# A fused attention and two-layer feed-forward kernel: the second layer's input weights kept as two words, its output weights split on VectorE

## The chip, the cores and the metric

The program runs on one core of one Trainium2 chip. The metric is the device time of one execution in microseconds (us); lower is better. The engines are TensorE (PE, with PEld for its weight loads), VectorE (DVE), ScalarE (ACT), GpSimd (POOL) and SyncE (SP), which issues almost all DMAs from one in-order queue.

## The reference, cut to what matters

```python
def _attn_ref(q, k, v, tau):                      # 4 x 8 heads, 576 rows of 64
    scores = scale * np.matmul(q, k.transpose(0, 1, 3, 2))
    scores = np.where(scores >= np.max(scores, -1, keepdims=True) - tau, scores, -1e9)
    ... softmax ...
    return np.matmul(attn, v)

def _moe_ref(x, w_in, w_out, g_ln):               # 2304 tokens, 512 -> 1024 -> 512
    h = x @ w_in
    solu = h * softmax(h)
    ln = (solu - mean) / sqrt(var + 1e-6) * g_ln
    return ln @ w_out

def _moe2_ref(x, w_in, w_out):                    # 2304 tokens, 512 -> 2048 -> 512
    h = x @ w_in
    g = h * np.tanh(log1p(exp(h)))
    return g @ w_out
```

The output is `_moe2_ref(_moe_ref(_attn_ref(...)))`. The change lies in the weights of `_moe2_ref`, called W2_in and W2_out here.

## The kernel before

**Precision.** A float32 product is made of three products of a shorter matmul type: every operand is split into a high word (a rounding copy, made by ScalarE) and a low word (operand minus high word), and high by high, low by high and high by low are summed.

**The second feed-forward layer** multiplies 2 by 2 blocks with seven products instead of eight (Strassen's scheme in Winograd's form). So each group of 256 columns of W2_in (`x` = 0, group `g` of 8) and each group of 256 rows of W2_out (`x` = 1) is first turned into seven block sums.

**Staging of the weights** (the loop over `g`, `x` and the half `k`; 32 units in all). One unit is two conversions from 64-bit floats (`convert`, with lines L491 on ScalarE, L494, L499, L500 and L502 on VectorE, L507 on GpSimd), then four sums of 128 x 128 on VectorE (L555), then a store of the seven block sums to DRAM (`w2c`). The constant `RAW = (0,1)` says for which weights these sums are stored as they are, as one word of 448 KB per unit (L558). For a weight that is not in `RAW`, `words7` would make two words of them at once: a ScalarE copy (L538), a subtraction (L539) and two stores (L541).

**The first layer's output y** goes the same way: block sums by L866 and L871 into the buffer `ys`, split into `yh` and `ys` (L538, L539, in parts of 1024 and 768 columns), stored to `yc`. Here `ys` and `yh` lie in the pool `mo`.

**The second layer** runs in five visits of 768 tokens. `ff_in` makes 256 hidden columns with seven products (A, the block of W2_in, by y); `mish` (L999) and four differences (L1003, every fourth line's worth on GpSimd, the others on VectorE) follow; each of seven results is split into `gh` (ScalarE, L1029) and `gl` (VectorE, L1031). `ff_out` multiplies these by B, the block of W2_out, and adds the results to `acc` (L1065 on ScalarE, L1067 on VectorE). Every product stands in the trace under L946 as `hoa` or `hob`, by the bank that it fills. `load_w` brings one block in: 128 KB from `w2c` (L969), a copy on ScalarE (L970) and a subtraction (L972). The table `SPLIT` sets that subtraction on VectorE for A (140 blocks) and on GpSimd for B (112 blocks).

**What sets the order.** All work is recorded as tasks; a planner (`Plan`) lists them by a cost for each and writes one fixed order for each engine. In its rules GpSimd's tasks and VectorE's tasks marked `port` don't run at the same time. The numbers of buffers (`NA` to `NF`) bound how far loads run ahead. A task "-" opens pools: `o_c` closes the pools of the first layer, `mo` among them, and opens `fc`, where B, `acc` and some of y's buffers lie; it waits for the last stores of y (`YST`). The instructions of the planned part follow each other across stages, so the second layer's first products stand between the last ones of the first layer.

Of the kernel before, what the change touches and what calls it, by code (L numbers as in the profile page):

```python
# [9 lines left out]
F32R = mybir.dt.float32r  # L10
# [301 lines left out]
def kernel(  # L312
# [34 lines left out]
    TU = 3 * PN  # L347
    TH = TU // 2
    NU = NT // TU
    RAW = (0,1)  # L350
    NQ = KF2 // 2
    XB = 2, 1, 2, 2
    WARM = 11
# [13 lines left out]
    def act(n, psum=False):  # L367
        return max(0.05 + n / 1200, 0.232) if psum else 0.094 + n / 1200
# [18 lines left out]
    part = [dram.tile([KD, 128, TU], F32, name=f"part{u}") for u in range(NU)]  # L387
    w2c = [[dram.tile([128, 7, 1 if x in RAW else 2, 256], F32, name=f"w2c{x}{g}") for g in range(NQ)] for x in range(2)]
    xd = [dram.tile([DM, S], F32, name=f"xd{i}") for i in range(B)]
# [4 lines left out]
    V, SC, G, TE = nc.vector, nc.scalar, nc.gpsimd, nc.tensor  # L394
    D = nc.sync.dma_start

    def buf(p, tag, shape, dtype=F32, bufs=1):
        return Buf(lambda: P[p], tag, shape, dtype, bufs)
# [134 lines left out]
    def words7(eng, e, cost, hi, x, t, dst, n, split):  # L533

        out = []
        for c in split:
            m = n * (c.stop - c.start)
            a = add("ACT", act(m), lambda c=c: SC.activation(hi.tile[:, c], f(x.tile[:, c]), ACTF.Copy), [t], [] if out else [hi], [hi, x])  # L538
            b = add(e, cost(m), lambda c=c: eng.tensor_tensor(x.tile[:, c], f(x.tile[:, c]), f(hi.tile[:, c]), ALU.subtract), [a], use=[hi, x], port=True)  # L539
            out.append((a, b))  # L540
        return [add("SP", dma(128 * 7 * n * 4), lambda w=w, y=y: D(dst(w), f(y.tile)), [o[w] for o in out], use=[y]) for w, y in ((0, hi), (1, x))]  # L541
# [4 lines left out]
    for g in range(NQ):  # L546
        for x, src in enumerate((w2_in, w2_out)):
            WST[x, g] = []
            for k in range(2):
                ws, wh, ts = b_ws.new(), b_wh.new() if x not in RAW else None, []  # L550
                for j in range(2):
# [4 lines left out]
                t = chain("DVE", [add7(3, 4, 6, ALU.add), add7(2, 3, 0, ALU.subtract), add7(5, 1, 2, ALU.subtract), add7(4, 0, 4, ALU.subtract)], ts, use=[ws], port=True)  # L556
# [24 lines left out]
    def opens(fn, deps):  # L581

        return add("-", 0.0, fn, deps)
# [169 lines left out]
    b_em = buf("mo", "em", [128, 2, 512], F32)  # L753
    b_so = buf("mo", "so", [128, 2, 512], F32, 2)
    b_ln = [buf("mo", n, [128, KF, PN], F32R) for n in ("LH", "LL")]
    b_ys, b_yh = buf("mo", "ys", [128, 7, 256], F32R), buf("mo", "yh", [128, 7, 256], F32R)
    b_s1 = buf("small", "ln", [128, 16], F32, 3)
    XSP, XSL, SO, ZT, TEV, YST, Y0, YS = ({} for _ in range(8))

    def x_split(t):  # L760
        XSL[t] = xh, xl = b_xh.new(), b_xl.new()
# [80 lines left out]
    def moe_y(p, j):  # L842
        lh, ll = LN[p]
        c, half = divmod(j, 2)
        cs = slice(c * 128, (c + 1) * 128)
        if half == 0:
            Y0[p, c, "y"] = b_two.new()
        y = Y0[p, c, "y"]
        ks = range(half * KF // 2, (half + 1) * KF // 2)

        def go(k):
            for x, (l, r) in enumerate(((W2H, lh), (W2L, lh), (W2H, ll))):
                TE.matmul(y.tile[:, :PN], l[:, k, cs], r.tile[:, k], start=(k == 0 and x == 0), stop=(k == KF - 1 and x == 2))  # L853

        deps = TEV[p] + [W2T[k, c * 128 // CW * CW] for k in ks]
        t = Y0.get((p, c))
        for k in ks:
            t = add("PE", pe(3, PN), lambda k=k: go(k), deps + ([t] if t else []), [] if t else [y], [lh, ll, y])
        Y0[p, c] = t
        if half == 0:  # L860
            return
        if c == 0:
            YS[p] = b_ys.new(), []
        ys, ts = YS[p]
        j, k = divmod(c, 2)
        ts.append(add("ACT", act(PN, True), lambda: SC.activation(  # L866
            f(ys.tile)[:, j:j + 5:4, k * 128:k * 128 + 128], y.tile[:, :PN].rearrange("p (a b) -> p a b", a=2), ACTF.Copy),
            [t], [] if c else [ys], [y, ys], order=ts[:1]))
        if c < KD - 1:
            return  # L870
        sub = lambda o, a, b: (dve(256), lambda: V.tensor_tensor(*(f(ys.tile[:, z]) for z in (o, a, b)), ALU.subtract))  # L871
        t = chain("DVE", [sub(3, 4, 0), sub(2, 5, 3), sub(4, 5, 4), sub(6, 1, 2)], ts, use=[ys], port=True)
        u, z = divmod(p, TU // PN)
        dst = lambda w: yc[u].rearrange("c q w z k n -> q c w z (k n)")[:, :, w, z]
        YST[p] = words7(V, "DVE", dve, b_yh.new(), ys, t, dst, 256, HALVES)


# [29 lines left out]
    for kind, t, k in pieces:  # L907
        moe_h(t, k) if kind == "h" else moe_y(t, k) if kind == "y" else moe_t(t)

    NA, NB, NL, NR, NX, NC, NF = 9, 22, 14, 15, 3, 6, 9  # L910

    def open_a():
        c3.close()
# [12 lines left out]

    o_a = opens(open_a, end_c3 + list(XST.values())[-2:] + [t for x in b_any.slots for t in x.users if t.eng != "PE"])
    o_b = opens(open_b, [o_a] + HT[-4:])
    o_c = opens(open_c, [o_b] + [t for ts in YST.values() for t in ts][-4:] + [t for ts in TEV.values() for t in ts][-16:])
    ff = [Bank(lambda n=n: P[n], f"{n}{k}") for n, m in (("hoa", 6), ("hob", 2)) for k in range(m)]  # L930
    for k in ff:
        k.after = o_a if k in ff[:6] else o_c
# [159 lines left out]
                                      [CO[v, e, i, t] for t in range(2)], use=[AC[v, e, i]])  # L1092

    MINUS = [{'D': ('DVE', dve(TH)), 'P': ('POOL', gps(TH))}[k] for k in 'DPDD']
    SPLIT = ((V, "DVE", dve),(G, "POOL", gps))
    LOWP = ()
    for z, (_, qs) in enumerate(VISITS):
        load_y(z)
# [60 lines left out]
```

## Time and profile before

| | |
|---|---|
| three runs | 900.48, 902.16, 904.35 us; median 902.16 us |
| the profiled execution | 899.4 us, of which the span (first to last instruction) 897.5 us |
| TensorE | busy 850.5 us, 95% of the span |
| VectorE | busy 804.8 us, 90% |
| ScalarE | busy 644.9 us, 72% |
| GpSimd | busy 433.2 us, 48% |
| DMA | 166.95 MB, mean 186 GB/s |

The profiled execution lies 1.9 us above its span and 2.8 us below the median of the runs. An engine is busy while one of its instructions is recorded; records of neighbours on one engine overlap a little, so that six instructions in a row take less than six times one. The second layer's products fill the time from about 525 us on. The trace's last matmul ends at 893.6 us.

### The profile page before, as it was taken

Reading aid. Unit: us, or ns where it says so; the run is one execution under the profiler, and the core shown is the slowest. Engines: PE = TensorE matmul, PEld = TensorE weight load, DVE = VectorE, ACT = ScalarE, POOL = GpSimd, SP = SyncE. Lnnn points to the kernel's source line nnn. Section 1 sums busy time; section 2 is a strip of 40 time slices with the busy share of each in tenths; the row PEclk is TensorE's granted clock in tenths of the full one; section 3 lists DMA queues with packets and bytes.
Section 4 is the critical chain, followed back from the end, with each engine's and each line's share of the span. In section 5 each row is a group of like instructions: output and inputs, shape, how many; then the busy total and the mean of one; then the engine's idle time right before and its main releaser. Section 6 shows DMA issues by size and latency. Waiting matters only on the chain.

```text
span 897.5 us, 16969 instructions
## 1 busy us (share of the span) xinstructions
PE 850.5 (95%) x5419; PEld 737.8 (82%) x5419; DVE 804.8 (90%) x1820; ACT 644.9 (72%) x1492; POOL 433.2 (48%) x542
## 2 busy tenths in 40 slices
PE   7998999989999999999999987998999999999997
PEld 4554667777787987887888986988989999999997
DVE  7999799899989899899888999799999899898987
ACT  5988899877798878775665866675767765766551
POOL 2566867665766657453343326452343734512311
PEclk9999999999999999999999999999999999999999
DMA  7454544345635465366995578957946466475331
GB/s 223 140 163 151 179 132 121 104 124 184 185 113 178 144 182 168 106 200 206 369 324 166 168 230 293 356 179 215 325 154 200 132 185 256 144 264 194 118 95 71
DMA packets 139482, 166.95 MB, mean 186 GB/s; under 512 B 14832, under 2 KB 111104, under 8 KB 139392
## 3 DMA queue, kind: packets, MB, share of 16 engines
q1 hardware_dynamic: 139248, 165.86, 58.0%
q8 instruction: 43, 0.70, 0.3%
q14 instruction: 47, 0.39, 0.1%
q10 hardware_dynamic: 144, 0.00, 0.0%
HBM read 121.97 MB, written 43.85 MB: 185 GB/s over the span
## 4 chain that ended last, share of the span: by engine, by line
PE 48%; DVE 24%; ACT 7%; DMA 5%; issue 4%; POOL 2%; SPq 0%; DVEq 0%; ACTq 0%; POOLq 0%
PE hoa L946 16%; PE p_mo L853 6%; PE hob L946 6%; PE p_mo L783 6%; PE p_ta L732 5%; DMA A<-w2c 3%; PE p_ta L684 3%; PE st L649 3%; DVE gl L1031 3%; DVE ws L555 2%; PE st L640 2%; DVE acc L1067 2%; DVE gf L1003 2%; DVE A L972 2%; DVE e L659 2%
## 5 line engine op out<-in xcount | busy, mean ns | idle before, releaser
L946 PE MATMUL hoa<-gh,B 128*128 128x384 f32 x512 | 131.9, 337 | 6.0 <-DVE acc L1067 3.9
L972 POOL TENSOR_TENSOR B<-B 128x256 fp32r<-128x256 f32 x112 | 92.7, 852 | 76.2 <-ACT B L970 60.1
L659 DVE SCALAR_TENSOR_TENSOR e<-st,m,e 128x576 f32<-128x576 f32 x132 | 106.1, 811 | 12.3 <-ACT e L656 6.8
L946 PE MATMUL hoa<-y,A 128*128 128x384 f32 x534 | 107.2, 340 | 9.2 <-ACT gf L993 5.0
L655 DVE TENSOR_REDUCE m<-st 128x1 f32<-128x576 f32 x132 | 97.2, 750 | 18.7 <-PE st L649 9.1
L656 ACT ACTIVATE e<-st,m 128x576 f32<-128x576 f32 x132 | 96.5, 741 | 23.1 <-DVE m L655 22.6
L946 PEld LDWEIGHTS hoa<-y,A 128*128 128x128 f32 x534 | 92.8, 188 | 13.5 <-ACT gf L993 8.4
L946 PEld LDWEIGHTS hoa<-gh,B 128*128 128x128 f32 x512 | 91.9, 188 | 10.1 <-DVE acc L1067 6.0
L1031 DVE TENSOR_TENSOR gl<-gf,gh 128x384 fp32r<-128x384 f32 x168 | 97.2, 613 | 1.8 <-ACT gh L1029 1.6
L684 PE MATMUL p_ta<-ident,e 128*128 128x128 f32 x576 | 85.6, 277 | 9.6 <-DVE e L659 5.4
L507 POOL TENSOR_TENSOR ws<-cf,cl 128x256 uint32<-128x256 uint32 x64 | 55.0, 866 | 74.4 <-DVE cf L502 47.9
L684 PEld LDWEIGHTS p_ta<-ident,e 128*128 128x128 f32 x576 | 65.7, 140 | 29.3 <-issue 6.1
L658 POOL TENSOR_SCALAR m<-m,cs 128x1 f32<-128x1 f32 x144 | 52.0, 363 | 75.6 <-DVE m L655 63.3
L1003 POOL TENSOR_TENSOR gf<-gf 128x384 f32<-128x384 f32 x24 | 30.8, 1282 | 116.1 <-DVE gf L1003 106.1
L946 PE MATMUL hoa<-gl,B 128*128 128x384 f32 x256 | 85.9, 336 | 0.2 <-DVE gl L1031 0.2
L853 PE MATMUL p_mo<-LH,W2H 128*128 128x256 f32 x288 | 84.7, 294 | 0.5 <-ACT so L790 0.5
L853 PE MATMUL p_mo<-LH,W2L 128*128 128x256 f32 x288 | 81.3, 282 | 0.0
L853 PE MATMUL p_mo<-LL,W2H 128*128 128x256 f32 x288 | 81.3, 282 | 0.0
L999 ACT ACTIVATE gf<-gf 128x384 f32<-128x384 f32 x72 | 37.4, 523 | 60.5 <-DVE gf L996 59.9
L1029 ACT ACTIVATE gh<-gf 128x384 fp32r<-128x384 f32 x168 | 77.7, 513 | 3.1 <-POOL gf L1003 2.1
L1067 DVE TENSOR_TENSOR acc<-acc,hoa 128x384 f32<-128x384 f32 x108 | 58.4, 547 | 15.8 <-PE hoa L946 11.2
L972 DVE TENSOR_TENSOR A<-A 128x256 fp32r<-128x256 f32 x140 | 68.6, 508 | 2.9 <-ACT A L970 2.9
(127 smaller groups left out, 2429.7 us busy)
## 6 DMA issues: line engine op xcount, KB each, us to landing
y<-yc SPq DMA_DIRECT2D x26, 768.0 KB, 4.2
A<-w2c SPq DMA_DIRECT2D x140, 128.0 KB, 2.5
w2c<-ws SPq DMA_DIRECT2D x32, 448.0 KB, 7.3
B<-w2c SPq DMA_DIRECT2D x112, 128.0 KB, 3.1
cr<-w_in SPq DMA_DIRECT2D x48, 256.0 KB, 3.5
cr<-w_out SPq DMA_DIRECT2D x48, 256.0 KB, 3.6
yc<-yh SPq DMA_DIRECT2D x9, 896.0 KB, 5.3
yc<-ys SPq DMA_DIRECT2D x9, 896.0 KB, 7.4
```

Of the source, the lines that this page charges most:

```text
L507: return add("POOL", gps(CW), lambda: G.tensor_tensor(at(), wide(cf), wide(cl), ALU.add), [t4, t2], slots if order is None else [], [cl, c ...
L655: t = add("DVE", dve(S), lambda: V.tensor_reduce(m.tile[:, 2:3], x(), AX.XY, ALU.max, negate=True), [t], [m], [st])
L656: a = add("ACT", act(S, True) + 0.1, lambda: SC.activation(et(), x(), ACTF.Exp, bias=m.tile[:, 2:3]), [t], [e] if h == 0 else (), [st, m, ...
L659: t = add("DVE", dve(S) + 0.06, lambda: V.scalar_tensor_tensor(et(), x(), m.tile[:, 1:2], et(), ALU.is_ge, ALU.mult, accum_out=sr.tile[:, ...
L684: TE.transpose(tp.tile[:, k * 128:(k + 1) * 128], e.tile[:, o:o + 128], ident)
L783: TE.matmul(h.tile, l.tile[:, kt], r[:, kt, j * 512:(j + 1) * 512], start=(kt == 0 and x == 0), stop=(kt == KD - 1 and x == 2))
L853: TE.matmul(y.tile[:, :PN], l[:, k, cs], r.tile[:, k], start=(k == 0 and x == 0), stop=(k == KF - 1 and x == 2))
L946: TE.matmul(x.tile[:, :TH], l, r, start=new and n == 0, stop=stop and n == len(steps) - 1, skip_group_check=True)
L972: return w, add(n, cost(256), lambda: eng.tensor_tensor(w.tile[:, 1], f(w.tile[:, 1]), f(w.tile[:, 0]), ALU.subtract), [t], use=[w], port= ...
L1029: a = add("ACT", act(TH), lambda h=h, x=x: SC.activation(h.tile, full(x), ACTF.Copy), [first], [h], [h, x])
L1031: out[c] = h, l, add(e, cost(TH), lambda h=h, l=l, x=x, eng=eng: eng.tensor_tensor(l.tile, full(x), f(h.tile), ALU.subtract), [a, *deps], ...
L1067: d = add("DVE", dve(TH), lambda: V.tensor_tensor(to(), to(), fr(), ALU.add), deps + [CO.get((v, e, i, t))], use=[ac, x])
```

## The change

W2_in leaves `RAW`: its 16 staging units run `words7`, so that the seven sums are split once and stored as two words (2 x 448 KB), and a block of A is loaded as 256 KB, ready to use, without copy and subtraction. W2_out stays one word; the subtraction after its load moves from GpSimd to VectorE. y's buffers `ys` and `yh` move from the pool `mo` into `ws`, which stays open to the end, so that `o_c` has to wait only for the last copies into `ys` (`YL`) and no longer for y's stores. To make room, seven counts of buffers fall: A from 9 to 8, B from 22 to 20, `gl` from 14 to 13, `gh` from 15 to 14, the second ring of y from 3 to 2, `acc` from 6 to 5, `gf` from 9 to 8.

```diff
-    RAW = (0,1)
+    RAW = (1,)
...
-    b_ys, b_yh = buf("mo", "ys", [128, 7, 256], F32R), buf("mo", "yh", [128, 7, 256], F32R)
+    b_ys, b_yh = buf("ws", "ys", [128, 7, 256], F32R), buf("ws", "yh", [128, 7, 256], F32R)
...
+    YL = []
...
+        YL[:] = ts
         YST[p] = words7(V, "DVE", dve, b_yh.new(), ys, t, dst, 256, HALVES)
...
-    NA, NB, NL, NR, NX, NC, NF = 9, 22, 14, 15, 3, 6, 9
+    NA, NB, NL, NR, NX, NC, NF = 8, 20, 13, 14, 2, 5, 8
...
-    o_c = opens(open_c, [o_b] + [t for ts in YST.values() for t in ts][-4:] + [t for ts in TEV.values() for t in ts][-16:])
+    o_c = opens(open_c, [o_b] + YL + [t for ts in TEV.values() for t in ts][-16:])
...
-    SPLIT = ((V, "DVE", dve),(G, "POOL", gps))
+    SPLIT = ((V, "DVE", dve),(V, "DVE", dve))
```

The planner writes a new order on every engine. Three places of it follow. Lines of the changed kernel are higher by 1 from y's split on and by 2 from the planner's section on (L972 becomes L974, L1003 becomes L1005).

GpSimd, where the second layer begins. Before, the splits of B (L972) start here:

```order
L1003 TENSOR_TENSOR gf<-gf 128x384
L507 TENSOR_TENSOR ws<-cf,cl 128x2x128 x2
L972 TENSOR_TENSOR B_7464<-B_7464 128x256
L972 TENSOR_TENSOR B_7475<-B_7475 128x256
L972 TENSOR_TENSOR B_7501<-B_7501 128x256
L972 TENSOR_TENSOR B_7506<-B_7506 128x256
L972 TENSOR_TENSOR B_7511<-B_7511 128x256
```

In the changed kernel, at the same place:

```order
L507 TENSOR_TENSOR ws<-cf,cl 128x2x128 x2
L1005 TENSOR_TENSOR gf<-gf 128x384
L507 TENSOR_TENSOR ws<-cf,cl 128x2x128 x4
L1005 TENSOR_TENSOR gf<-gf 128x384 x3
L507 TENSOR_TENSOR ws<-cf,cl 128x2x128 x2
```

All 112 splits have left GpSimd; the last step of the weights' conversion (`ws<-cf,cl`) and 24 differences (`gf<-gf`) stay.

VectorE, in the second layer's opening. Before, the splits of A stand between the adds and splits of the hidden columns:

```order
L972 TENSOR_TENSOR A_7327<-A_7327 128x256
L972 TENSOR_TENSOR A_7339<-A_7339 128x256
L996 TENSOR_TENSOR gf<-gf,hoa_7332 128x384
L972 TENSOR_TENSOR A_7357<-A_7357 128x256
L1031 TENSOR_TENSOR gl<-gf,gh 128x384 x4
```

In the changed kernel:

```order
L974 TENSOR_TENSOR B_7216<-B_7216 128x256
L998 TENSOR_TENSOR gf<-gf,hoa_6977 128x384
L974 TENSOR_TENSOR B_7230<-B_7230 128x256
L974 TENSOR_TENSOR B_7233<-B_7233 128x256
L1005 TENSOR_TENSOR gf<-gf 128x384
L974 TENSOR_TENSOR B_7258<-B_7258 128x256
L1033 TENSOR_TENSOR gl<-gf,gh 128x384
```

The splits of A are gone from VectorE's row and those of B stand in it, with the adds and splits behind them.

SyncE's queue of DMAs, at the first loads of B. Before, they come behind the last stores of y (`yc_59`), whose landing `o_c` awaits:

```order
L541 DMA yc_59<-yh 128x7x256
L541 DMA yc_59<-ys 128x7x256
L969 DMA A_7396<-w2c_66 128x256
L969 DMA A_7405<-w2c_66 128x256
L969 DMA A_7446<-w2c_66 128x256
L969 DMA B_7464<-w2c_71 128x256
```

In the changed kernel a store of W2_out's unit precedes them, and the last two stores of y come 36 entries further down:

```order
L975 DMA A_7106<-w2c_65 128x512
L975 DMA A_7121<-w2c_65 128x512
L481 DMA cr<-w_in 128x512
L558 DMA w2c_75<-ws 896x1x128
L971 DMA B_7216<-w2c_71 128x256
```

The first loads of B moved ahead of those stores, and A's loads are twice as wide.

## Rows read from the trace of the kernel before

**Rows 1.** Busy time by stretch: PE, PEld, DVE, ACT, POOL, clock, DMA share, GB/s.

```profile
0.00:525.00 525.00, 500.31 (x3458) 399.30 (x3459) 468.67 (x1142) 414.35 (x901) 294.27 (x389) 1.00 0.57 176
525.00:575.00 50.00, 42.68 (x231) 39.32 (x230) 43.04 (x85) 31.64 (x82) 22.97 (x28) 0.97 0.89 307
575.00:750.00 175.00, 164.72 (x918) 158.06 (x917) 168.22 (x356) 118.58 (x311) 77.48 (x84) 1.00 0.63 198
750.00:893.60 143.60, 142.76 (x818) 141.16 (x816) 124.35 (x240) 80.30 (x200) 38.44 (x44) 1.00 0.50 167
```

**Rows 2.** What PE waited for from 525 us on: total us, times, longest.

```profile
PE hoa L946 <- ACT gf L993: 6.1, 5, 2.8
PE hoa L946 <- DVE acc L1067: 3.9, 5, 1.3
PE hoa L946 <- DVE gf L996: 3.8, 3, 2.1
```

**Rows 3.** VectorE's timeline, with nothing of POOL beside it: start, us, count last.

```profile
540.81 0.28 DVE L555 TENSOR_TENSOR ws<-ws 128x128 f32<-128x128 f32 x1
601.28 0.54 DVE L1003 TENSOR_TENSOR gf<-gf 128x384 f32<-128x384 f32 x1
610.35 1.08 DVE L972 TENSOR_TENSOR A<-A 128x256 fp32r<-128x256 f32 x3
611.35 0.55 DVE L1031 TENSOR_TENSOR gl<-gf,gh 128x384 fp32r<-128x384 f32 x1
```

**Rows 4.** Timeline of POOL, DVE and PE in the second layer's opening.

```profile
545.81 7.33 POOL L972 TENSOR_TENSOR B<-B 128x256 fp32r<-128x256 f32 x9 [0.45 <-ACT B L970]
...
548.63 0.82 DVE L555 TENSOR_TENSOR ws<-ws 128x128 f32<-128x128 f32 x1
...
557.16 1.16 PE L946 MATMUL hoa<-y,A 128*128 128x384 f32 x4 [2.14 <-DVE gf L996]
```

**Rows 5.** Timeline of ACT and PE some microseconds earlier; in brackets idle time and releaser.

```profile
534.05 0.42 ACT L970 ACTIVATE A<-A 128x256 fp32r<-128x256 f32 x1 [0.43 <-DMA A<-w2c]
...
534.90 1.33 PE L946 MATMUL hoa<-y,A 128*128 128x384 f32 x6 [2.80 <-ACT gf L993]
```

**Rows 6.** Groups of the whole trace: count, busy us, mean ns, idle before.

```profile
L972 POOL TENSOR_TENSOR B<-B 128x256 fp32r<-128x256 f32 x112 | 92.7, 852 | 76.2 <-ACT B L970 60.1 <-DMA B<-w2c 8.5 <-issue 4.8
...
L970 ACT ACTIVATE A<-A 128x256 fp32r<-128x256 f32 x140 | 55.0, 410 | 10.9 <-DMA A<-w2c 9.5 <-PE hoa L946 1.0
...
L539 DVE TENSOR_TENSOR ys<-ys,yh 128x1024 fp32r<-128x1024 f32 x9 | 11.5, 1275 | 0.0
...
L539 DVE TENSOR_TENSOR ys<-ys,yh 128x768 fp32r<-128x768 f32 x9 | 10.0, 1107 | 0.0
```

**Rows 7.** Busy time of L972 (DVE, POOL), L1003 (DVE, POOL) and L507 (POOL), 575 to 750.

```profile
575.00:750.00 175.00, 35.60 (x70) 47.16 (x57) 1.00 0.63 198
...
575.00:750.00 175.00, 27.25 (x33) 15.95 (x11) 1.00 0.63 198
...
575.00:750.00 175.00, 14.91 (x16) 1.00 0.63 198
```

**Rows 8.** VectorE's groups from 575 to 750 us.

```profile
L1031 DVE TENSOR_TENSOR gl<-gf,gh 128x384 fp32r<-128x384 f32 x74 | 43.3, 617 | 1.5 <-ACT gh L1029 1.5
...
L1003 DVE TENSOR_TENSOR gf<-gf 128x384 f32<-128x384 f32 x33 | 27.2, 826 | 0.8 <-ACT gf L999 0.8
...
L555 DVE TENSOR_TENSOR ws<-ws 128x128 f32<-128x128 f32 x32 | 13.0, 415 | 0.0
```

**Rows 9.** What VectorE waited for from 525 us on, for A's splits.

```profile
DVE A L972 <- ACT A L970: 2.9, 3, 1.8
```

**Rows 10.** Busy time in the opening's second half, columns as in rows 1.

```profile
550.00:575.00 25.00, 22.07 (x116) 20.92 (x115) 18.67 (x34) 13.38 (x36) 13.30 (x18) 0.93 0.99 377
```

**Rows 11.** DMA issues: count, KB each, median us from issue to landing.

```profile
A<-w2c SPq DMA_DIRECT2D x140, 128.0 KB, 2.5
...
cr<-w_in SPq DMA_DIRECT2D x48, 256.0 KB, 3.5
```

## The prediction

> **What bounds the kernel now.** I read the busy time by stretch first, then TensorE's waits, then VectorE's rows in the stretches where TensorE waits, then GpSimd's rows beside them.
>
> The stretches say where there is something to win [rows 1]. Up to 525 us TensorE is busy for 500.3 us, and the instructions that the change touches are mostly staging. From 750 us on it is busy for 142.8 of 143.6 us: nothing is left there. Between lie the opening of the second layer (525 to 575 us, TensorE 42.7 of 50) and what I call the middle (575 to 750 us, 164.7 of 175), where VectorE is busy for 168.2 us, 96%. The idle time of TensorE is 7.3 us in the opening and 10.3 us in the middle. That is all that a faster second layer can give back, apart from the 3.9 us behind the last matmul.
>
> TensorE's waits from 525 us on have three large releasers [rows 2]: the ScalarE copy out of PSUM (L993, 6.1 us), `acc` (L1067, 3.9 us) and the add L996 (3.8 us), the last two on VectorE. Products wait because the instruction that empties their bank stands late in an in-order queue.
>
> Why is VectorE late? With nothing beside them, a 128-column operation takes 0.28 us, one of 384 columns 0.54 to 0.55, and three splits of A 1.08, or 0.36 each [rows 3]. While GpSimd runs nine splits of B back to back (7.33 us, 0.81 each), the same 128-column operation takes 0.82 us [rows 4]: it sits out one of GpSimd's instructions. The add L996 that TensorE needs stands behind a dozen such instructions, and TensorE is idle for 2.14 us [rows 4]. So a split of B on GpSimd is not free for VectorE.
>
> **The change part by part, opening.** Removed: GpSimd's splits of B and the queue in which VectorE sat them out; with them goes the 2.14 us. The other long gap, 2.80 us, ends with a copy L993 that stands on ScalarE behind a copy of A, which was waiting for A's DMA [rows 5]. A's copies are removed, so this copy no longer stands behind a DMA. What is late next is the product's own block of A, straight from the DMA; I take 2.0 of the 2.80. Loads of B no longer wait for y's last stores; what they feed was waiting for other things too, and I count nothing. Gross: 4.1 us.
>
> Against it stands the DMA. From the seventh store of y to the first store of `acc`, the new order's DMAs move 31.0 MB, the old one's 26.5 (A's blocks doubled, staging in two words). In the opening's second half the DMA engines are already busy for 0.99 of the time at 377 GB/s [rows 10]. At that rate 4.5 MB are 12 us if nothing gives way, and nothing if they fall into the idle shares around it (0.89 in the whole opening, 0.63 behind it, [rows 1]). I take 1.1, near the lower end, since the stretch is over 100 us long and B's loads are now spread ahead of it. Opening: **-3.0 us**, bounds -7.3 and +8.
>
> A single load of A doubles. Loads of 128 KB land in 2.5 us, those of 256 KB in 3.5 [rows 11], so it lands about 1.0 us later but saves the copy (0.41 us, [rows 6]) and the split (0.36). It stays hidden while a slot is free early: in the middle 918 matmuls, 153 products of six, fill 175 us [rows 1], 1.14 us for one, and about every second one frees a slot of A. Eight slots are still over 15 us of work ahead of a load of 3.5 us. For the same reason I cost the other lower counts at nothing; if that cover is gone, each late `gl` costs 0.55 us.
>
> **Middle, VectorE's sum.**
> - 70 splits of A go [rows 7]: between 70 x 0.36 = 25.2 us and the recorded 35.6 us, which holds their own time behind GpSimd. I take 30.
> - 57 splits of B come: 57 x 0.36 = 20.5 us.
> - What GpSimd's splits of B cost the others: L1031 took 617 ns instead of 550 (74 times, 5.0 us), L1003 826 instead of 540 (33 times, 9.4 us), L555 415 instead of 280 (32 times, 4.3 us) [rows 3, 8]. Of these 18.7 us I give B its share of GpSimd's busy time, 47.2 of 78.0 us [rows 7]: 11.3 us. The bounds are 0 and the whole 47.2.
> - Staging: in the new order 18 units' sums precede the last split `LL` of the first layer, before 21, so three units come later; one falls into the opening, two into the middle. A unit has twelve short operations, 12 x 0.28 = 3.4 us; two are 6.8. Five or so of the sixteen two-word splits fall here too. One has 896 columns, between 1.11 us (768) and 1.28 us (1024) [rows 6], so 1.2 each and 6.0 us.
>
> Together -30 + 20.5 - 11.3 + 6.8 + 6.0 = -8.0 us: VectorE falls from 168.2 to about 160 us of 175. It also gets a new wait. A split of B stands in VectorE's queue, behind ScalarE's copy and the load, with adds and `gl` behind it, and TensorE behind those. GpSimd waited 60.1 us for these copies at no cost [rows 6]. VectorE's splits of A had the same wait and it was 2.9 us for 140 of them [rows 9], so 112 of B should cost about 2.3 us, less than what goes. TensorE's own 164.7 us stay. Of 8.0 us I let half arrive, because part of its waiting hangs on ScalarE and on the order: **-4.0 us**, bounds -10.3 and +8.
>
> **Early part.** Ten two-word splits before the first `gl` add 12 us to VectorE, ten copies on ScalarE at most 3.5 x 0.41 = 1.4 us each. Three units (10.2 us) and 19 splits of A (6.8 us) leave. The new stores hold the staging buffers longer, but nobody else needs those. TensorE's idle 24.7 us there [rows 1] hang on attention's and the first layer's own chains. I take **0**, plus or minus 3 for another order. ScalarE's load falls throughout; it bounds nothing.
>
> **Sum.** 899.4 - 3.0 - 4.0 = 892.4 us for an execution like the profiled one. The median of the runs stands 2.8 us above that execution, so 895.2 us.
>
> **The rivals.**
> - *The waits form again.* TensorE is near its own work everywhere, and a wait that VectorE no longer ends may be ended by ScalarE's copies out of PSUM or by the order of products. For it: L993 is the largest releaser [rows 2]. Against it: the gaps that I named stand directly behind work that goes. Time: about 901 us.
> - *The DMA in the opening*, the slower one. If A's wider loads and the doubled stores meet the stretch that is at 0.99 [rows 10], TensorE waits for A itself. Of the 12 us some 8 would arrive, and they eat the gain: 895.2 + 8 + 3 = 906 us, over 907 with all 12. It decides from the point where 25 us of the opening ask for more than 9.4 MB (377 GB/s).
> - *VectorE becomes the bound.* If what VectorE lost beside GpSimd fell on staging with time to spare, only the plain counts matter: in the middle -25.2 + 20.5 + 6.8 + 6.0 = +8.1 us on an engine that is 96% busy. That gives 902.2 + 8 = 910 us. For it: L555 and the conversions are among the delayed. Against it: L1003 and L1031 are too, with the larger sum [rows 8], and TensorE waits for what stands behind them. The Trainium skill has a rule that points this way ("Perfetto Trace Analysis", section "Optimizing Scalar/DVE Operations"): where VectorE is saturated, offloading work to ScalarE or even GpSimd may make sense, which is the opposite of moving B's splits to VectorE. The same passage warns that the two share an SBUF port, so that moving work between them might not help; the trace's 0.28 and 0.82 us side with the warning.
> - *More than I count.* If the 96% in the middle is what holds TensorE, all 8 us arrive and the opening gives its 7.3: 902.2 - 15 = 887 us.
>
> **How the numbers follow.** Chances: my forecast 0.55, waits that form again 0.20, DMA 0.10, VectorE 0.07, more than counted 0.08. A change under 0.5%, 4.5 us, can hardly be told from none here. Faster than 897.7 us: nearly nine tenths of the forecast, all of the larger gain, a fifth of the first rival, 0.60. Slower than 906.7 us: half of the DMA case and nearly all of VectorE's, with a little from the others, 0.13. The rest is 0.27. The forecast's own range, with the early part's 3 us and half of the other bounds, is 889 to 901. The range of 8 in 10 reaches to 886, just past the larger gain, and to 906, into the DMA case.
>
> **What would show it.** Right: in the changed trace VectorE's `gl` and L1003's differences (L1033, L1005 there) come down towards 0.55 us on average, TensorE's idle time in the opening and the middle falls from 17.6 us to about 11, and no wait of TensorE names a load of A. Wrong, by the DMA: a DMA share of 0.95 and more over the whole opening, with TensorE released by A's loads. Wrong, by VectorE: its busy share in the middle stays at 95%, and the splits of B there wait for ScalarE's copies for more than some 5 us. If TensorE's idle time falls as said and the time does not, the early part has taken it: its 24.7 us of idle would have grown. What makes all of it void is a planner's order that differs for reasons that none of these rows shows.

## The result and the profile after

The changed kernel takes 891.38 us (median of four runs, 889.64 to 893.76) against 901.89 us before (900.48 to 904.35). The ratio is 0.9885, with a 95% interval of 0.9855 to 0.9914: about 10.5 us faster, where 7 were predicted. The profiled execution took 889.64 us, of which the span is 887.9.

The busy time by stretch of the changed kernel, in the columns of [rows 1]:

```profile
0.00:525.00 525.00, 496.00 (x3414) 392.37 (x3415) 460.43 (x1080) 409.57 (x871) 286.65 (x381) 1.00 0.57 179
525.00:575.00 50.00, 47.30 (x285) 46.09 (x284) 48.45 (x114) 36.39 (x90) 8.00 (x7) 1.00 0.99 343
575.00:750.00 175.00, 171.42 (x976) 168.54 (x975) 167.97 (x402) 107.71 (x259) 35.16 (x34) 1.00 0.91 304
750.00:884.00 134.00, 131.70 (x751) 129.52 (x749) 104.47 (x216) 63.42 (x151) 8.56 (x8) 1.00 0.62 207
```

TensorE's idle time falls from 7.3 to 2.7 us in the opening and from 10.3 to 3.6 in the middle. Up to 525 us it rises, from 24.7 to 29.0. VectorE is as busy in the middle as before (168.0 against 168.2 us), but for 402 instructions instead of 356, while TensorE gets 976 matmuls done instead of 918.

What TensorE waited for from 525 us on in the changed kernel, against [rows 2]:

```profile
PE hoa L948 <- ACT gf L995: 3.1, 5, 1.5
PE hoa L948 <- DVE gl L1033: 1.3, 1, 1.3
PE hob L948 <- DVE gl L1033: 1.2, 1, 1.2
PE hoa L948 <- DVE acc L1069: 0.9, 2, 0.6
```

The add (L998 now) is gone from the head of the list, the other two releasers of [rows 2] have shrunk, and no wait names a load of A. VectorE's groups from 575 to 750 us, against [rows 8]:

```profile
L1033 DVE TENSOR_TENSOR gl<-gf,gh 128x384 fp32r<-128x384 f32 x79 | 41.2, 556 | 0.3 <-ACT gh L1031 0.3
...
L1005 DVE TENSOR_TENSOR gf<-gf 128x384 f32<-128x384 f32 x36 | 26.5, 737 | 0.5
...
L974 DVE TENSOR_TENSOR B<-B 128x256 fp32r<-128x256 f32 x56 | 24.5, 460 | 0.0
...
L555 DVE TENSOR_TENSOR ws<-ws 128x128 f32<-128x128 f32 x44 | 13.9, 316 | 0.0
```

The same instructions are shorter: `gl` 617 to 556 ns, the differences 826 to 737, the staging sums 415 to 316.

To see where the time went I cut each trace at one event, the start of the last matmul into `p_mo` (the first layer's last product), and call the rest, up to the last matmul, the second layer. Idle is the sum of gaps between recorded matmuls. "Clock" is the most that stretches at a granted clock of 0.50 can have cost in the first and in the second part, half their length (last section). Ratios are to runs of the kernel before taken with each kernel.

| kernel | median us | ratio (95%) | first layer ends | second layer | idle in it | clock, first + second |
|---|---|---|---|---|---|---|
| before | 901.9 | | 527.6 | 366.0 | 18.4 | 0 + 1.7 |
| after | 891.4 | 0.9885 (0.9855 to 0.9914) | 533.0 | 351.0 | 7.7 | 0 + 0 |
| e1 | 887.1 | 0.9847 (0.9822 to 0.9871) | 528.2 | 350.0 | 7.9 | 1.7 + 1.7 |
| e2 | 887.1 | 0.985 (0.9824 to 0.9876) | 530.4 | 351.1 | 8.8 | 3.4 + 1.7 |
| e3 | 907.9 | 1.0092 (1.0069 to 1.0114) | 534.6 | 369.8 | 20.9 | 1.7 + 3.4 |
| e4 | 887.6 | 0.9866 (0.9844 to 0.9888) | 534.3 | 347.6 | 6.3 | 3.4 + 0 |
| e5 | 885.5 | 0.9845 (0.9818 to 0.9871) | 529.4 | 350.8 | 8.0 | 0 + 0 |
| e6 | 903.0 | 1.0027 (1.0003 to 1.005) | 532.3 | 363.7 | 15.1 | 0 + 5.1 |
| e7 | 890.2 | 0.989 (0.9867 to 0.9914) | 533.7 | 350.2 | 6.7 | 0 + 0 |
| e9 | 891.6 | 0.992 (0.9888 to 0.9951) | 533.8 | 351.1 | 8.0 | 5.1 + 0 |
| e10 | 911.0 | 1.009 (1.0063 to 1.0116) | 539.9 | 365.3 | 17.8 | 5.1 + 1.7 |
| e11 | 901.0 | 0.9992 (0.9978 to 1.0007) | 529.3 | 365.5 | 20.0 | 0 + 1.7 |
| e12 | 891.8 | 0.9895 (0.9869 to 0.9921) | 543.5 | 347.5 | 5.1 | 8.5 + 3.4 |
| e13 | 887.2 | 0.9838 (0.9817 to 0.9859) | 535.4 | 344.4 | 3.3 | 3.4 + 0 |

The change gains 15.0 us in the second layer and loses 5.4 in the part before it. The prediction had 7.0 and 0. The cut doesn't divide the same work in every kernel: 78 of the second layer's 2016 matmuls stand before it in the kernel before and in e1, e2, e7 and e11, 72 in e6 and e13, 66 in the others. Twelve matmuls take about 2.1 us there, so for equal work the change gains about 17 us and loses about 7.5. Each row of the table rests on one profiled execution, the ratios on all runs.

### The profile page after: what moved, and what is told of

It reads as the page before. It is cut to its first block, busy times and chain, and to the rows that moved or that the text cites. A ratio compares the mean times of both kernels' runs of the same rounds, so it can differ in the third digit from the quotient of the medians.

```text
span 887.9 us, 16722 instructions
## 1 busy us (share of the span) xinstructions
PE 846.4 (95%) x5419; PEld 736.5 (83%) x5419; DVE 781.9 (88%) x1808; ACT 617.1 (70%) x1368; POOL 338.4 (38%) x430
## 4 chain that ended last, share of the span: by engine, by line
PE 49%; DVE 19%; ACT 9%; DMA 8%; issue 4%; POOL 3%; SPq 1%; POOLq 0%; DVEq 0%; ACTq 0%
PE hoa L948 21%; PE hob L948 7%; PE p_mo L784 4%; PE p_ta L732 4%; PE p_mo L854 4%; PE p_ta L684 3%; DMA B<-w2c 3%; DVE e L659 3%; PE st L649 2%; DVE m L655 2%; ACT e L656 2%; PE st L640 2%; DVE cf L502 2%; DVE gl L1033 1%; DMA w2c<-ws 1%
## 5 line engine op out<-in xcount | busy, mean ns | idle before, releaser
L948 PE MATMUL hoa<-y,A 128*128 128x384 f32 x648 | 125.7, 336 | 1.1 <-ACT gf L995 1.1
L948 PE MATMUL hoa<-gh,B 128*128 128x384 f32 x484 | 123.5, 336 | 1.2 <-DVE acc L1069 0.9
L948 PEld LDWEIGHTS hoa<-y,A 128*128 128x128 f32 x648 | 112.6, 188 | 2.7 <-ACT gf L995 2.6
L1005 POOL TENSOR_TENSOR gf<-gf 128x384 f32<-128x384 f32 x24 | 27.6, 1152 | 214.2 <-DVE gf L1005 211.0
L507 POOL TENSOR_TENSOR ws<-cf,cl 128x256 uint32<-128x256 uint32 x64 | 61.1, 964 | 113.7 <-DMA w2c<-ws 59.9
L1033 DVE TENSOR_TENSOR gl<-gf,gh 128x384 fp32r<-128x384 f32 x168 | 88.9, 567 | 0.7 <-ACT gh L1031 0.7
L948 PEld LDWEIGHTS hoa<-gh,B 128*128 128x128 f32 x484 | 87.0, 188 | 2.8 <-DVE acc L1069 1.9
L948 PE MATMUL hoa<-gl,B 128*128 128x384 f32 x242 | 81.0, 335 | 1.3 <-DVE gl L1033 1.3
L1069 DVE TENSOR_TENSOR acc<-acc,hoa 128x384 f32<-128x384 f32 x101 | 54.1, 547 | 14.7 <-PE hoa L948 12.8
L784 PE MATMUL p_mo<-W1H,XH 128*128 128x512 f32 x144 | 60.6, 421 | 2.8 <-DVE LL L839 2.8
L854 PEld LDWEIGHTS p_mo<-LH,W2H 128*128 128x128 f32 x288 | 55.0, 191 | 2.0 <-ACT ys L867 1.1
```

Of the source, the lines that this page charges most:

```text
L507: return add("POOL", gps(CW), lambda: G.tensor_tensor(at(), wide(cf), wide(cl), ALU.add), [t4, t2], slots if order is None else [], [cl, c ...
L784: TE.matmul(h.tile, l.tile[:, kt], r[:, kt, j * 512:(j + 1) * 512], start=(kt == 0 and x == 0), stop=(kt == KD - 1 and x == 2))
L948: TE.matmul(x.tile[:, :TH], l, r, start=new and n == 0, stop=stop and n == len(steps) - 1, skip_group_check=True)
L1033: out[c] = h, l, add(e, cost(TH), lambda h=h, l=l, x=x, eng=eng: eng.tensor_tensor(l.tile, full(x), f(h.tile), ALU.subtract), [a, *deps], ...
L1069: d = add("DVE", dve(TH), lambda: V.tensor_tensor(to(), to(), fr(), ALU.add), deps + [CO.get((v, e, i, t))], use=[ac, x])
```

## Experiments

**GpSimd's splits of B cut short, nothing else moved (e1).** The kernel before, in its own order; B's splits are cut to 8 of 256 columns, so B's low words are left out. A split so cut still takes 0.35 us, so GpSimd's busy time in the middle falls by 25 us (77.5 to 52.5) and not by the whole 47.2 of the splits.

```diff
-            return w, add(n, cost(256), lambda: eng.tensor_tensor(w.tile[:, 1], f(w.tile[:, 1]), f(w.tile[:, 0]), ALU.subtract), [t], use=[w], port=True)
+            m = 8 if x == 1 else 256
+            return w, add(n, cost(256), lambda: eng.tensor_tensor(w.tile[:, 1, :m], f(w.tile[:, 1, :m]), f(w.tile[:, 0, :m]), ALU.subtract), [t], use=[w], port=True)
```

> The kernel before, in its own order on every engine; only GpSimd's 112 splits of B are cut from 256 columns to 8, so the low words of B are left out. Theory G (GpSimd's splits of B hold VectorE, and that is most of what the second layer lost): 5 to 10 us faster than before, 892 to 897 us, the mean of the gl splits (L1031) in the second layer falls from some 0.60 us towards 0.56, and TensorE's idle time from 525 us on falls from 18 us to 10 or less. Theory A (the gain comes from A's copies and splits that went): less than 2 us. Theory O (the gain comes from the planner's new order and the earlier opening, not from any one engine's load): less than 2 us.

Measured: 1.5% faster, more than I expected, and a second layer of 350.0 us, which is already the changed kernel's. The middle and VectorE's groups in it:

```profile
575.00:750.00 175.00, 172.56 (x987) 170.46 (x986) 158.63 (x375) 123.53 (x323) 52.53 (x85) 1.00 0.71 231
```

```profile
L1032 DVE TENSOR_TENSOR gl<-gf,gh 128x384 fp32r<-128x384 f32 x82 | 44.4, 575 | 1.5 <-ACT gh L1030 1.5
L973 DVE TENSOR_TENSOR A<-A 128x256 fp32r<-128x256 f32 x70 | 29.5, 440 | 1.5 <-ACT A L970 1.5
...
L1004 DVE TENSOR_TENSOR gf<-gf 128x384 f32<-128x384 f32 x36 | 23.6, 656 | 1.3 <-ACT gf L1000 1.1
...
L555 DVE TENSOR_TENSOR ws<-ws 128x128 f32<-128x128 f32 x32 | 8.8, 284 | 0.0
```

With the order the same, what VectorE lost beside GpSimd's B can be read off against [rows 7, 8]: `gl` 74 x 0.042 = 3.1 us, the differences 33 x 0.170 = 5.6, the staging sums 32 x 0.131 = 4.2, and the 70 splits of A 35.6 - 29.5 = 6.1. Together 19.0 us of the middle's 175, for shortening the splits and not for removing them; the prediction gave the whole of them 11.3. The trace of the kernel before says the same of the unchanged kernel: from 515 to 890 us, the 135 of 168 `gl` with no instruction of GpSimd beside them take 544 to 559 ns, and the 33 others 873 ns on average and up to 1373. For the differences on VectorE it is 544 to 559 ns for 34 and 929 on average for 38.

Could the gain come instead from B being ready sooner? TensorE's wait for these splits in the kernel before, from 525 us on, was too small for that:

```profile
PE hoa L946 <- POOL B L972: 0.9, 2, 0.4
```

In e1, of TensorE's waits from 525 us on, those for `acc` and for the add [rows 2] are gone and the copies' are left:

```profile
PE hoa L946 <- ACT gf L994: 6.4, 5, 3.2
```

**The B part of the change alone (e7).** The kernel before with B's splits on VectorE; the planner writes its own order.

```diff
-    SPLIT = ((V, "DVE", dve),(G, "POOL", gps))
+    SPLIT = ((V, "DVE", dve),(V, "DVE", dve))
```

> The kernel before with B's splits on VectorE beside A's; the planner makes its own order. The other part of the change alone. Shared budget: a split of B held VectorE for up to 0.81 us from GpSimd and takes 0.36 us on VectorE itself, so 112 of them give back up to some 40 us of VectorE's time: 3 to 10 us faster than before, 890 to 897 us. If VectorE is simply the bound by its own instructions: 5 us slower or more, 905 us and up.

Measured: 0.989, as much as the whole change gains (0.9885), from this one line. The middle:

```profile
575.00:750.00 175.00, 172.49 (x984) 169.92 (x984) 172.19 (x433) 124.32 (x324) 42.80 (x28) 1.00 0.71 233
```

```profile
L972 DVE TENSOR_TENSOR B<-B 128x256 fp32r<-128x256 f32 x60 | 24.6, 427 | 0.0
L1003 DVE TENSOR_TENSOR gf<-gf 128x384 f32<-128x384 f32 x36 | 22.9, 636 | 0.3 <-ACT gf L999 0.3
```

VectorE takes 24.6 us of splits more, gets most of that back (at least 19.0 us by e1), and is busy for 98% of the middle. TensorE nonetheless gets 66 more matmuls through. A busy share of 96% before was therefore no sign that VectorE had no room: part of it was waiting for GpSimd, recorded as work.

**The cost of B on VectorE (e4), and GpSimd burdened again (e3).** Both in the changed kernel's own order. e4 cuts the splits as e1 does, so B's low words are left out. e3 puts a subtraction on GpSimd behind each split, which leaves B's low words zero:

```diff
+            def split():
+                eng.tensor_tensor(w.tile[:, 1], f(w.tile[:, 1]), f(w.tile[:, 0]), ALU.subtract)
+                G.tensor_tensor(w.tile[:, 1], f(w.tile[:, 1]), f(w.tile[:, 1]), ALU.subtract)
```

> The changed kernel in its own order, with VectorE's 112 splits of B cut to 8 columns (B's low words left out). It prices what the splits cost where they now stand. Theory G: VectorE has slack enough now that TensorE sets the pace, 0 to 3 us faster than the changed kernel, 888 to 891 us. If VectorE still bounds the second layer: 4 us or more faster, under 887.5.

> The changed kernel in its own order, with a GpSimd subtraction of 256 columns put behind each of the 112 splits of B (in place; it leaves B's low words zero). GpSimd's load is that of before again, VectorE keeps its own instructions. Theory G: 5 to 10 us slower than the changed kernel, 896 to 901 us, the mean of the gl splits above 0.60 us again. Theories A and O: within 2 us of the changed kernel's 891.4.

Measured: e4's second layer is 3.4 us shorter than the changed kernel's. A split cut to 8 columns still takes 172 ns, so VectorE's time for the 112 of them falls from 46.5 to 17.0 us: 29.5 us of it are worth 3.4 us there. The totals, 0.9866 and 0.9885, can't be told apart. e3 is 2.1% slower than the changed kernel (1.0092 against 0.9885), more than expected. Its middle and its waits of TensorE from 525 us on:

```profile
575.00:750.00 175.00, 162.96 (x908) 158.08 (x907) 170.22 (x388) 104.37 (x253) 75.85 (x85) 0.99 0.87 292
```

```profile
PE hoa L948 <- ACT gf L998: 10.2, 6, 3.4
PE hob L948 <- DVE acc L1072: 4.1, 3, 2.7
```

Busy GpSimd brings back the waits of [rows 2], the copies and `acc` first. The run has a weakness that I saw too late: the added instruction also stands between the split and the products of its block, so the 2.1% hold that delay too, although no wait of TensorE from 525 us on names that instruction. It bears the theory out and gives no price.

**A's copies and splits cut short (e2), and with loads of 256 KB (e11).** The kernel before, in its order; both cut ScalarE's copy and VectorE's split of A to 8 columns, so A's low words are left out. e11 also lets each load bring 256 KB, the same words twice; its order still reckons with 128 KB.

```diff
-            t = add("SP", dma(128 * 1024), lambda: D(f(w.tile[:, 1]), w2c[x][g][:, c, 0]), WST[x, g] + [gate], [w])
+            t = add("SP", dma(128 * 1024), lambda: D(f(w.tile), w2c[x][g][:, c].broadcast_to([128, 2, 256])) if x == 0 else D(f(w.tile[:, 1]), w2c[x][g][:, c, 0]), WST[x, g] + [gate], [w])
```

> The kernel before, in its own order; A's 140 copies on ScalarE and 140 splits on VectorE are cut to 8 columns, and the products read the loaded word of A for both words, so A's low words are left out. Theory G: VectorE loses some 25 to 30 us of work in the middle but GpSimd still holds it, 2 to 5 us faster than before, less than with GpSimd's splits cut. Theory A: 6 to 12 us faster, more than with GpSimd's splits cut. Theory O: less than 2 us.

> The kernel with W2_in's copies and splits cut to 8 columns (so W2_in's low words are left out, 887.1 us), with one more thing: each load of a W2_in unit brings 256 KB instead of 128 KB (the same words twice), as the change's loads do. If the doubled loads cost nothing by themselves, it is within 2 us of that: 885 to 889. If the transfers were what took the gain of W2_in's part away, it loses several us: 892 or more, with waits of TensorE on the loaded tile in the stretch behind 525 us.

Measured: e2 gains as much as e1, more than any of the three theories expected, though GpSimd is busy for 76.3 us of its middle. So either relief of VectorE is enough to bring the second layer to about 350 us; neither engine's work alone was the cause. e11 loses all of it again (0.9992). ScalarE's waits for A's loads from 515 to 890 us, in e2 and then in e11:

```profile
ACT A L972 <- DMA A<-w2c: 15.9, 27, 2.2
```

```profile
ACT A L972 <- DMA A<-w2c: 49.2, 60, 2.6
```

TensorE's largest releaser in e11, from 515 us on, is not the loaded block, as expected, but what stands behind these copies in ScalarE's queue:

```profile
PE hoa L946 <- ACT gf L994: 7.8, 8, 3.2
PE hob L946 <- ACT gf L994: 5.2, 4, 2.2
```

and the loads take longer to land in the same stretch, in e2 and in e11:

```profile
A<-w2c SPq DMA_DIRECT2D x126, 128.0 KB, 2.4
```

```profile
A<-w2c SPq DMA_DIRECT2D x125, 256.0 KB, 3.9
```

So the doubled loads are not cheap by themselves. 1.5 us more for one load goes with a loss of 1.4%, some 13 us, where an in-order engine stands waiting for it, in an order that was written for the shorter one. The doubled traffic also slows other loads (those of B from 2.9 to 4.1 us), so not all of the 13 us need come from A's; but ScalarE's waits for B's loads stay the same (5.6 and 5.8 us) while those for A's grow by 33 us. The changed kernel has no copy of A, so only TensorE uses the block, and no wait of TensorE from 525 us on names one.

**The change without the B part (e6), and without both parts on the weights (e10).** The changed kernel with B's splits on GpSimd again; e10 also sets W2_in back to one word, so that y's place, the smaller buffer counts and the gate are what is left.

```diff
-    SPLIT = ((V, "DVE", dve),(V, "DVE", dve))
+    SPLIT = ((V, "DVE", dve),(G, "POOL", gps))
```

> The changed kernel with B's splits on GpSimd, as before; the planner makes its own order. One part of the change undone. If VectorE and GpSimd share one budget and either relief alone restores the second layer (as the two cuts in the order of before suggest): the second layer takes 350 to 354 us from the first layer's last matmul, the whole 888 to 895 us. If B's move to VectorE is needed: 360 us or more, the whole 898 us or more.

> The change without its two parts on the weights: y's last buffers stand beside the staging buffers with the change's counts and its gate, W2_in is stored once and split on both engines' copies as before, GpSimd has W2_out's splits and ScalarE W2_in's copies. If the y buffers' place matters in itself (fewer transfers waiting in the opening, or a gate that comes earlier or later), it stands apart from the kernel before by more than 5 us: 893 to 897. If the place only made room, the time is that of before: 899 to 905, with the second layer's stretch after the first layer's last product at 363 to 369 us against 366.0 before, since VectorE shares its operand path with all of GpSimd's splits and does all of W2_in's.

Measured: e6 is 0.3% slower than the kernel before, e10 0.9% slower. Against expectation, e2's gain doesn't come with the two-word storage. e6's middle shows what ate them:

```profile
575.00:750.00 175.00, 167.44 (x933) 162.37 (x932) 165.88 (x345) 106.99 (x259) 82.41 (x90) 0.99 0.89 297
```

```profile
L1033 DVE TENSOR_TENSOR gl<-gf,gh 128x384 fp32r<-128x384 f32 x78 | 49.7, 678 | 0.1
...
L1005 DVE TENSOR_TENSOR gf<-gf 128x384 f32<-128x384 f32 x35 | 26.8, 767 | 0.4
...
L555 DVE TENSOR_TENSOR ws<-ws 128x128 f32<-128x128 f32 x48 | 18.8, 393 | 0.0
...
L539 DVE TENSOR_TENSOR ws<-ws,wh 128x896 fp32r<-128x896 f32 x6 | 7.2, 1207 | 0.0
```

A's 35.6 us are gone, but 48 staging sums instead of 32 and six two-word splits have moved in (5.8 and 7.2 us more), and `gl` takes 678 ns instead of 617 beside a GpSimd that is busier than before. VectorE is as full as it was. e10's 911.0 us lie outside both ranges expected. Its second layer is that of before, as expected if the place only made room (365.3 us), and the loss lies in the part ahead of it, 12.3 us, of which 5.1 is the clock.

By the ratios, in per cent of the time before: y's place with its counts +0.9 (e10), W2_in's two words on top of it -0.6 (e10 to e6), B's splits on top of both -1.4 (e6 to the changed kernel), and B's splits from the kernel before -1.1 (e7). So the first two roughly cancel, and a gain like the whole change's comes with B alone. Each of these kernels has its own order, so the +0.9 is y's place, the counts and that order together.

**The two-word splits (e5), and another order (e9).** e5: the changed kernel in its order, with the sixteen units' copies and splits cut to one of seven chunks; the unsplit sum is stored as both words, so the bytes are the same and W2_in's low words are left out. e9: the changed kernel with one constant of the planner changed, which writes another order.

```diff
-    TURNS = 40
+    TURNS = 15
```

> The changed kernel in its own order; the sixteen two-word splits of W2_in in the staging are cut to one block of seven on ScalarE and on VectorE, and both stores take the unsplit sums (same bytes, W2_in's low words are wrong). It asks why the first layer ends at 533 us in the changed kernel and at 528 before. Theory S (the added splits hold the first part up): the first layer's last matmul comes at 527 to 530 us, the whole 4 to 6 us faster than the changed kernel. Theory P (the planner's other order of the first part does it): it stays at 532 to 535 us, the whole within 2 us of the changed kernel.

> The changed kernel with 15 of the planner's 40 turns, so that another of its orders is taken (every engine's row differs, the work is the same). Theory P: the first layer's end moves by 2 us or more against 533 us, either way, and the whole with it, 886 to 900 us. Theory S: the first layer's end stays within 1 us of 533 us, since the same splits are there.

Measured: without the two-word splits the first layer ends 3.6 us earlier (529.4), the second layer is unchanged (350.8) and the ratio is 0.9845 where the changed kernel has 0.9885 (the intervals just overlap). In the other order the second layer takes 351.1 us, so the gain doesn't hang on one order. Its first layer ends at 533.8, but up to 5.1 us of that is the clock, which cost the changed kernel nothing; so e9 doesn't show the loss to be independent of the order.

Where the loss lies can be read from attention's last product with V, in the kernel before and in the changed one:

```profile
L732 PE MATMUL p_ta<-ey,V x256: 432/432/483, 30.2 to 412.8; 128*64 128x320 f32 x128
L732 PE MATMUL p_ta<-ey,V x256: 432/432/484, 29.3 to 418.6; 128*64 128x320 f32 x128
```

It starts 5.8 us later, behind the same number of matmuls (2758), so attention has already lost all of it. Less the clock, the kernels in the order of before (with e1, e2, e11) come to this product at 412.4 to 413.7 us, those in the changed kernel's (e3, e4, e5 with it) at 416.5 to 418.6, and e9 at 415.2. From there to the first layer's end the changed order takes 114.4 to 114.8 us with the two-word splits and 111.1 without (e5); so the splits' price of about 3.5 us holds against three traces, and it falls behind attention. In attention e5 is as late as the changed kernel (418.3), so the time of the splits isn't what is lost there. The planner's order in attention remains, with the doubled stores of the staging, which e5 keeps; e7 has no such stores and its first layer still ends at 533.7. Which move of the order costs the time is not shown.

**VectorE given all the differences (e12 on e7, e13 on the changed kernel).** GpSimd's quarter of the differences goes to VectorE too.

```diff
-    MINUS = [{'D': ('DVE', dve(TH)), 'P': ('POOL', gps(TH))}[k] for k in 'DPDD']
+    MINUS = [{'D': ('DVE', dve(TH)), 'P': ('POOL', gps(TH))}[k] for k in 'DDDD']
```

> The kernel before with W2_out's splits on VectorE alone (890.2 us) and with the quarter of the staged sums' differences that GpSimd has left taken to VectorE as well, so GpSimd does nothing but memory clears in the second layer. VectorE gives some 28 differences of about 0.5 us for as many stretches of over 1 us in which GpSimd held its operands. If that sharing is what is left of the cost, it gains 1 to 4 us: 886 to 889. If VectorE's count is now the bound (it was busy 172.2 of 175 us in the middle), it loses: 891 to 896.

> The changed kernel (891.4 us) with the same edit: the quarter of the staged sums' differences that GpSimd has is taken to VectorE. VectorE was busy 168.0 of 175 us in the middle and TensorE idle 7.7 us in the whole second layer. If what GpSimd's remaining differences hold of VectorE is worth more than their count, 887 to 890; if not, 891 to 895. It can't gain more than the 7.7 us.

Measured: e13 is the fastest version that computes all of it, 887.2 us. The middle and the differences in it:

```profile
575.00:750.00 175.00, 173.57 (x990) 171.03 (x990) 166.63 (x413) 109.83 (x264) 21.66 (x20) 1.00 0.92 312
```

```profile
L1005 DVE TENSOR_TENSOR gf<-gf 128x384 f32<-128x384 f32 x48 | 25.1, 551 | 0.3
```

48 differences now take 25.1 us where 36 took 26.5. VectorE has more instructions and less busy time. The second layer is 6.6 us shorter than the changed kernel's, about 1 us of it for six matmuls that stand before the cut. Its ratio and the changed kernel's (0.9838 and 0.9885) were not taken together and their intervals just touch. e12 gains 2.7 us in the second layer over e7, with twelve matmuls more in it, and nothing in the total (0.9895 and 0.989); its median lies in the range expected if VectorE's count were the bound. Its profiled execution was its slowest, 896.75 us against a median of 891.76, with up to 11.9 us lost to the clock, so neither its first part nor that range decides anything.

## Why the prediction was right, and where its sizes were wrong

The sign and the mechanism were right, and the time lies in the range; it came out 3.8 us below the forecast, and that it came so close is luck: two errors of 8.0 and 5.4 us cancel in part. The range itself was narrower than its own rule: the early part's 3 us and half of the other bounds, added up, give 887 to 910 us, not 889 to 901. What was forecast as the right signs came only in part: `gl` came down to 556 ns but the differences only to 737, and TensorE's idle time in the opening and the middle fell to 6.3 us, not to about 11.

- **What GpSimd's splits cost VectorE** was given 11.3 us in the middle, by B's share of GpSimd's busy time. e1 measured 19.0 for splits that were only shortened. The step looked at three kinds of instruction and left A's own delay to the removal of A; but also by the three alone, 12.9 us, B's share of the loss was larger than its share of the time. The splits of B that came were put too low: 57 at 0.36 us, 20.5, where 56 took 24.5. The 0.36 is a third of three records that overlap; one split alone takes 0.41 us.
- **"Half arrives"** was the step that failed most. The prediction let 4.0 of 8.0 us reach TensorE in the middle. Its idle time there fell by 6.7, and in the opening by 4.6 where the net term was 3.0. In e1, e2, e4, e5, e7, e9 and the changed kernel the second layer comes to 347.6 to 351.1 us, whichever of VectorE's burdens is removed. The reason given for halving, that part of the waiting hangs on ScalarE, didn't carry it: in e1 the waits for ScalarE's copies do stay (6.4 us), and those for VectorE, which go, are enough for 350 us. Nor did VectorE's busy time fall to 160 us; it stayed at 168.0, with 46 instructions more done in it. So a fall in VectorE's busy time was the wrong measure of what reaches TensorE. For the second layer the rival *more than I count* was right in size: 15 us there, and 15.0 measured.
- **The 2.14 us gap** [rows 4] was counted at its length. It cost up to 1.7 us more, since TensorE worked at the lower clock behind it; the 0.93 in [rows 10] was that.
- **The early part**, 0 plus or minus 3, lost 5.4 us. The sign that the prediction named for this, idle time above 24.7 us, is there: 29.8 us up to the first layer's last product. The two-word splits, which were seen (12 us on VectorE) and set against work that leaves, cost about 3.5 us behind attention (e5). Attention itself lost 5.8, more than the 3 us allowed for another order; it comes with the new order or with the doubled stores, and which move costs the time stays open. The twelve matmuls that moved behind the cut hide some 2 us of the two.
- **The new wait on VectorE** for ScalarE's copies of B was put at 2.3 us, with 5 as the point from which it would matter. From 515 us on it was

```profile
DVE B L974 <- ACT B L972: 4.5, 6, 1.6
```

twice the estimate, still below that point.
- **The DMA rival** fell, though its own sign appeared: the DMA share is 0.99 over the whole opening. TensorE waited for no load of A. A's loads landed later than the 3.5 us estimated, and B's later than their 3.1 us in the kernel before:

```profile
A<-w2c SPq DMA_DIRECT2D x140, 256.0 KB, 4.4
B<-w2c SPq DMA_DIRECT2D x112, 128.0 KB, 4.0
```

The price in that rival was real all the same; e11 shows it (1.4%) where a copy on ScalarE waits for the load. The share of the DMA engines was the wrong sign here: the two kernels differ in whether an in-order engine waits behind the transfer.
- **The waits form again** fell too: the ScalarE copy is still TensorE's largest releaser, but with 3.1 us instead of 6.1.
- **VectorE becomes the bound** fell clearest, though its first sign appeared: VectorE was busy for 96% of the middle as before. That share was no sign of a bound. e7 gave a VectorE that was 96% busy 60 more instructions in the middle and the kernel became 1.1% faster. The Trainium skill's advice to take work off a saturated VectorE, even to GpSimd ("Perfetto Trace Analysis", section "Optimizing Scalar/DVE Operations"), would have led the other way here; its warning in the same place, that the two share a port, is what e1, e3 and e13 agree with.

## What to carry to other kernels

A busy share near 100% on VectorE may be time in which its instructions stand behind GpSimd's: compare one instruction's duration with nothing beside it and in the crowded stretch before deciding who is full, and then move work onto VectorE if the difference, summed, is about as large as the work. When a DMA grows, look for the in-order engine that consumes it, not only at the DMA share. And where a planner writes the order, a part of a change can cost time in a stretch far from its target, here in attention: try each part alone, since here one line gave as much as the whole and the other two roughly cancelled.

## What the runs showed of the hardware

The granted clock halves behind some of TensorE's gaps, and the price comes in steps of one size. The kernel before around the gap of [rows 4], in stretches of 1 us (columns of [rows 1]):

```profile
555.00:556.00 1.00, 0.03 (x1) 0.00 (x0) 1.00 (x3) 0.00 (x0) 1.00 (x3) 1.00 1.00 382
556.00:557.00 1.00, 0.00 (x0) 0.00 (x0) 1.00 (x2) 0.00 (x0) 1.00 (x2) 1.00 1.03 414
557.00:558.00 1.00, 0.84 (x4) 0.84 (x5) 0.38 (x2) 0.86 (x3) 0.98 (x2) 0.89 1.04 426
558.00:559.00 1.00, 0.96 (x3) 0.45 (x2) 0.69 (x2) 1.00 (x4) 0.00 (x0) 0.50 1.01 423
559.00:560.00 1.00, 0.91 (x3) 0.92 (x4) 1.00 (x3) 0.91 (x4) 0.00 (x0) 0.50 1.02 423
560.00:561.00 1.00, 1.00 (x5) 1.00 (x4) 0.10 (x1) 0.26 (x1) 0.00 (x0) 0.50 1.00 404
561.00:562.00 1.00, 1.00 (x7) 1.00 (x6) 0.00 (x0) 0.62 (x2) 0.00 (x0) 0.91 1.05 426
```

TensorE does nothing for 2 us, then works at 0.50 (1.2 GHz of its 2.4) for about 3.4 us, which is 1.7 us lost if it has work all the time. Every stretch at 0.50 between the first and the last matmul of the 14 traces lasts 3.4 us or twice that, so the losses in the table are multiples of 1.7 us: none in the changed kernel's, e5's and e7's profiled executions, one before, four in e10, seven in e12. Not every gap does it: the 2.80 us of [rows 5] left the clock at 1.00, as did 3.20 us in e11, while e4's clock fell behind one of 1.20. What decides is not shown. Runs of one kernel differ by it: e12's six runs go from 889.5 us at a mean clock of 0.996 to 896.8 at 0.987.
